# GpSimd's weight subtractions one per block of products, and zero matmuls in TensorE's idle time of the search

## The chip, the cores and the metric

The kernel runs on one core of a Trainium2 chip. The metric is the device time of one execution in microseconds (us); less is better. Engines are named as in the profile: PE is TensorE (PEld its weight loads), DVE is VectorE, ACT is ScalarE, POOL is GpSimd, SP is SyncE, which issues most of the DMAs.

## What is computed

A gated linear attention over 32 heads feeds a mixture of experts, in which tokens are assigned to experts greedily over all pairs (the reference, cut):

```python
batch, n_heads, seq, head_dim = (4, 8, 768, 48)      # 3072 tokens of 384 features
for t in range(S):
    state = alpha[:, :, t, :, None] * state + einsum('bhd,bhe->bhde', k[:, :, t], v[:, :, t])
    y[:, :, t] = einsum('bhd,bhde->bhe', q[:, :, t], state)
...
N, D, E, F = (3072, 384, 8, 1024)
logits = x @ w_gate
order = argsort(-logits.flatten())                   # best (token, expert) pairs first
for idx in order:
    tok, e = idx // E, idx % E
    if assigned[tok] >= 0 or counts[e] >= N // E:    # at most 384 tokens for each expert
        continue
    assigned[tok] = e; counts[e] += 1
for e in range(E):
    h = maximum(x[mask_e] @ w1[e], 0)                # w1[e] is 384x1024
    out[mask_e] = h @ w2[e]                          # w2[e] is 1024x384
```

## The kernel before

The program is recorded first and ordered afterwards. Each operation is handed to a `Plan` (`pl.add(engine, cost, fn, r=..., w=...)`) with an assumed cost, what it reads and what it writes. `Plan.order` lays all operations out in a simulated time by these costs, by priorities (`pl.base`: an earlier expert and an earlier block rank higher) and by buffers that come free; `Plan.issue` emits them in that order. On the chip each engine runs its own instructions strictly in the order emitted and waits on semaphores for the others. So a changed cost or a new dependency moves instructions on all engines.

The run has three stages.

1. Attention: 24 steps of four chunks of 128 tokens. The last products of a step on PE are those of the function `intra`. Behind the last step stand on PE only transposes, logits (L452, L460) and the counts of `choice` (L520).
2. Search and assignment. The greedy order is replaced by eight rounds. A round finds the next expert that becomes full, and its threshold, digit by digit. In one step of a round DVE compares the tokens' digits with all possible values (`cmp`, L638), PE counts with 24 small matmuls (L668), DVE makes `g` (L671), PE broadcasts it by one matmul (L675), DVE takes `k` (L677) and the next digit `nd` (L680). `update` (L730 to L760) then moves the tokens of the full expert to their next choice. `extract` makes the row numbers of the round's tokens (`hot` L804, PE's pick L810, `idx` L813), and POOL gathers the rows with three indirect DMAs (`xr`, L818).
3. The experts. For each of the eight experts the 1024 hidden features are done in eight blocks of 128. `prep` transposes the gathered rows on PE (L887) and splits them into a rounded part `xh` (ACT, L889) and a rest `xl` (DVE, L891). A block (`ffn1`) takes three products of three matmuls each into a PSUM tile `s` (L905; there are two of them): `w1h` with `xh`, `w1h` with `xl`, `w1l` with `xh`. ACT takes the relu (`hh`, L909), DVE its rest (`hl`, L910). `ffn2` (L927) multiplies by `w2` two blocks later, into the tiles `y`, `lg` and `xt`. The result is copied by ACT (`yo`) and scattered to the output by POOL (L937).

From the second round on, rounds and experts overlap: while the blocks of one expert run, the round of the next is searched, and on PE the counts stand between the products.

`split` prepares the weights, half an expert (four blocks) at a time. ACT rounds `w1r` to `w1h` (L861). POOL takes the rest, `w1l = w1r - w1h` (L866), in one subtraction of 128x384 elements per block, 64 in all. The rest of `w2` is made by ACT (L870) and an accumulating DMA that POOL issues (`w2l`, L874). POOL's queue thus holds the subtractions, the gathers `xr`, the `w2l` DMAs and the scatters, in one order. A subtraction may run as soon as its weights are loaded and rounded and one of three half-expert buffers of `w1l` is free. The `Plan` knows the operations marked `port=True` (the subtractions, `cmp`, `hot`): in its simulated time these never overlap.

Of the kernel before, what the change touches and what calls it, by code (L numbers as in the profile page):

```python
# [35 lines left out]
class Plan:  # L36


    def __init__(self):
        self.ops, self.writer, self.readers, self.base, self.free = [], {}, {}, 0.0, {}  # L40

# [97 lines left out]
    def issue(self):  # L139
        self.prev = {}  # L140
        for i in self.order():
            self.ops[i][2]()
            self.prev[self.ops[i][0]] = i


HOP = {"PE": 0.3, "DVE": 0.15, "ACT": 0.2, "POOL": 0.2, "SP": 2.2}
OVER, SELF = {"DVE": 0.09}, {"DVE": 0.035}
# [4 lines left out]
def gla_moe_kernel(ctx, tc, q, k, v, alpha, w_gate, w1, w2, out):  # L152
    nc = tc.nc
# [178 lines left out]
    def step(s):  # L332
# [103 lines left out]
        for a in range(2):  # L436
            def intra(a=a):
                for u in (2 * a, 2 * a + 1):
                    for h in range(2):
                        nc.tensor.matmul(yb.t[64 * h:64 * h + D, u], rv.t[:, u, h], sm.t[:, h, u],  # L440
                                         start=False, stop=(u == 3), skip_group_check=True)
            add(P_, 0.44, intra, r=[sm, rv], w=[yb], mode=48)
        add(A_, 0.6, lambda: nc.scalar.activation(yt.t, yb.t, AF.Copy), r=[yb], w=[yt])
# [181 lines left out]
    scattered, stores = [], set()  # L625
    gap = rw.tile([128, 1], F32, name="gap")

    def v_(cost, fn, r=(), w=(), port=False):
# [224 lines left out]
    def split(i, hf, raw):  # L853
# [4 lines left out]
        for a in range(2):  # L858
# [4 lines left out]
            for b in range(2):  # L863
                c2 = slice(a * w_ + b * 128, a * w_ + b * 128 + 128)
                pl.base = at(i, 4 * hf + 2 * a + b)
                add(G_, 1.08, lambda c2=c2: nc.gpsimd.tensor_sub(l1.t[:, :, c2], r1.t[:, :, c2], h1.t[:, :, c2]),  # L866
                    r=[r1, (h1, a)], w=[(l1, 2 * a + b)], port=True)
            q2 = slice(2 * a, 2 * a + 2)
# [9 lines left out]
    def prep(i, xr):  # L878
        xh, xl = pl.buf(XH), pl.buf(XL)
        pl.base = at(i) + 20.0  # L880
        for b in range(NB):
# [3 lines left out]
            def turn_rows(b=b, x=x):  # L885
                for d in range(DB):
                    nc.tensor.transpose(x.t[:, d], xr.t[:, b, d * 128:(d + 1) * 128], ident)  # L887
            add(P_, 0.33, turn_rows, r=[(xr, b)], w=[x], mode=128)
            add(A_, 0.49, lambda x=x, bs=bs: nc.scalar.activation(xh.t[:, :, bs], x.t[:, :DB], AF.Copy),  # L889
# [5 lines left out]
    def ffn1(i, q, w, xh, xl):  # L895
# [12 lines left out]
        src = lambda: o.t.rearrange("p a b -> p (a b)")[:, :CAP]  # L908
        add(A_, 0.49, lambda: nc.scalar.activation(hh.t, src(), AF.Relu), r=[o], w=[hh])  # L909
        v_(0.553, lambda: nc.vector.scalar_tensor_tensor(hl.t, src(), 0.0, hh.t, op0=OP.max, op1=OP.subtract),  # L910
# [107 lines left out]
```

## Time and profile before

| what | value |
|---|---|
| three runs | 511.98, 511.89, 509.33 us; median 511.89 |
| profiled execution, its own time | 509.61 us |
| its span, first to last instruction | 507.9 us |
| mean granted PE clock | 0.901 |
| PE / PEld / DVE busy | 412.1 / 366.4 / 301.6 us |
| ACT / POOL busy | 194.4 / 229.4 us |
| first product of an expert | 177.16 us |

Busy time is the sum of the intervals in which an engine's instructions ran; an instruction that is held up while it runs counts with its whole length. The granted clock (PEclk) is the share of full speed at which PE was allowed to run. A row of the timeline gives the start in us, the duration in us, the engine, the source line, the operation, output<-input, the shapes and how many of them stand in a row; in brackets follow the idle time of the engine before it and what ended that. A row of a group ends with the busy time in us and the mean of one in ns, and behind the bar the idle time before. A row of a table of windows gives the window, its length, the busy time and number of instructions of each engine, the granted clock, the DMAs' share and their GB/s.

### The profile page before, as it was taken

What the parts mean: (1) busy time and instruction counts of PE and PEld (TensorE: products, weight loads), DVE (VectorE), ACT (ScalarE), POOL (GpSimd) and SP (SyncE); (2) the same over time, 40 slices, a digit from 0 to 9 for tenths busy, and PEclk for the clock granted to TensorE, in tenths of its full rate; (3) what the DMA queues carried; (4) which work ended last, traced back from release to release, by engine and by line L of the source; (5) the groups of instructions that cost most, each with busy time, mean ns of one, the idle gap of its engine ahead of it and who ended that gap; (6) DMA issues with size and microseconds to landing.
All of it is one profiled execution on the core that took longest, in us unless ns stands there. A gap on an engine that the chain in (4) does not pass through costs nothing.

```text
span 507.9 us, 10573 instructions
## 1 busy us (share of the span) xinstructions
PE 412.1 (81%) x4134; PEld 366.4 (72%) x4134; DVE 301.6 (59%) x823; ACT 194.4 (38%) x351; POOL 229.4 (45%) x257
## 2 busy tenths in 40 slices
PE   4899999999832486995978868897869959889792
PEld 2778887788722375984977767796759949889691
DVE  6978878877468649558569568447666612021110
ACT  1456554555300431720631622533432434633211
POOL 5777776677100521580622920850470653630202
PEclk8799999999965559996999989899889989989997
DMA  8859977621010755943814914833841992433101
GB/s 301 307 190 310 305 233 218 174 94 64 3 63 0 203 157 124 286 109 107 255 31 122 300 22 89 317 62 63 298 107 22 318 361 63 108 63 62 48 0 46
DMA packets 37681, 76.28 MB, mean 150 GB/s; under 512 B 3584, under 2 KB 17920, under 8 KB 37632
## 3 DMA queue, kind: packets, MB, share of 16 engines
q1 hardware_dynamic: 32256, 53.60, 31.3%
q0 software_dynamic: 5376, 22.02, 18.1%
q8 instruction: 32, 0.52, 0.4%
q14 instruction: 17, 0.14, 0.1%
HBM read 53.59 MB, written 9.44 MB: 124 GB/s over the span
## 4 chain that ended last, share of the span: by engine, by line
PE 48%; DVE 23%; issue 15%; DMA 5%; POOL 5%; ACT 2%; SPq 0%; POOLq 0%; DVEq 0%; ACTq 0%
PE s L905 12%; DVE cmp L638 5%; PE s L389 4%; PE y L927 4%; PE y L440 4%; PE st L668 4%; PE y L433 3%; PE xt L377 3%; PE xt L927 3%; PE lg L927 3%; DMA xr<-x_dram,idx 3%; DMA w2r<-in_moe_w_dram 3%; PE lg L452 2%; POOL out_dram L937 2%; DVE te L349 2%
## 5 line engine op out<-in xcount | busy, mean ns | idle before, releaser
L910 DVE SCALAR_TENSOR_TENSOR hl<-s,hh 128x384 fp32r<-128x384 f32 x64 | 35.3, 554 | 93.7 <-ACT hh L909 61.4
L866 POOL TENSOR_TENSOR w1l<-w1r,w1h 128x384 fp32r<-128x384 f32 x64 | 68.1, 1242 | 37.8 <-ACT w1h L861 37.7
L909 ACT ACTIVATE hh<-s 128x384 fp32r<-128x384 f32 x64 | 31.4, 491 | 120.1 <-PE s L905 113.3
L937 POOL DMA_INDIRECT out_dram<-yo,idx x24 | 29.4, 1225 | 69.3 <-ACT yo L932 65.8
L905 PE MATMUL s<-xh,w1h 128*128 128x384 f32 x192 | 48.7, 365 | 8.3 <-DVE hl L910 5.4
L668 PEld LDWEIGHTS <-cmp 128*128 128x128 bf16 x816 | 30.5, 118 | 32.8 <-DVE cmp L638 27.0
L668 PE MATMUL st<-o,cmp 128*128 128x8 bf16 x816 | 33.1, 175 | 25.1 <-DVE cmp L638 18.2
L905 PE MATMUL s<-xh,w1l 128*128 128x384 f32 x192 | 48.8, 365 | 5.4 <-DVE hl L910 3.2
L905 PE MATMUL s<-xl,w1h 128*128 128x384 f32 x192 | 49.2, 367 | 4.7 <-ACT hh L909 2.6
L638 DVE TENSOR_TENSOR cmp<-nd,iota 128x1536 bf16<-128x1536 bf16 (+4 forms) x32 | 51.5, 1619 | 0.8
L818 POOL DMA_INDIRECT xr<-x_dram,idx x24 | 26.1, 1089 | 49.9 <-DVE idx L813 44.5
L874 POOL DMA_DIRECT2D w2l<-w2r x16 | 15.3, 956 | 73.5 <-ACT w2l L870 71.7
L905 PEld LDWEIGHTS s<-xh,w1h 128*128 128x128 f32 x192 | 36.3, 204 | 9.7 <-DVE hl L910 5.6
L905 PEld LDWEIGHTS s<-xh,w1l 128*128 128x128 f32 x192 | 36.1, 203 | 7.6 <-issue 6.5
L905 PEld LDWEIGHTS s<-xl,w1h 128*128 128x128 f32 x192 | 36.1, 204 | 7.0 <-ACT hh L909 3.9
L861 ACT ACTIVATE w1h<-w1r 128x768 fp32r<-128x768 f32 x32 | 26.0, 838 | 32.7 <-DMA w1r<-in_moe_w_dram 32.6
L359 POOL TENSOR_TENSOR kh<-rk,te 128x512 f32<-128x512 f32 (+1 forms) x24 | 29.4, 1229 | 18.0 <-DVE te L349 7.3
L389 PE MATMUL s<-qh,kh 64*128 64x128 f32 x384 | 31.0, 298 | 7.0 <-DVE qh L359 6.0
L392 POOL TENSOR_SCALAR_AFFINE_SELECT sm<-sm 128x1024 f32<-128x1024 f32 x24 | 26.8, 1116 | 17.9 <-ACT sm L391 16.3
L389 PEld LDWEIGHTS s<-qh,kh 64*128 64x128 f32 x384 | 25.0, 195 | 11.8 <-DVE qh L359 6.5
L359 POOL TENSOR_TENSOR qh<-rq,tp 128x512 f32<-128x512 f32 (+1 forms) x24 | 29.5, 1229 | 5.2 <-DVE tp L355 4.1
L349 DVE TENSOR_TENSOR_SCAN te<-al,z 128x511 f32<-128x511 f32 (+2 forms) x26 | 30.9, 1189 | 0.9
(190 smaller groups left out, 957.9 us busy)
## 6 DMA issues: line engine op xcount, KB each, us to landing
w1r<-in_moe_w_dram SPq DMA_DIRECT2D x16, 768.0 KB, 7.3
w2r<-in_moe_w_dram SPq DMA_DIRECT2D x16, 768.0 KB, 8.4
w2l<-w2r POOLq DMA_DIRECT2D x16, 768.0 KB, 6.1
al<-in_alpha_dram SPq DMA_DIRECT2D x24, 260.0 KB, 4.4
rk<-in_k_dram SPq DMA_DIRECT2D x24, 256.0 KB, 4.4
rq<-in_q_dram SPq DMA_DIRECT2D x24, 256.0 KB, 4.2
rv<-in_v_dram SPq DMA_DIRECT2D x24, 192.0 KB, 3.6
x_dram<-xg SPq DMA_DIRECT2D x6, 768.0 KB, 4.4
```

What stands on the lines that cost most here:

```text
L349: nc.vector.tensor_tensor_scan(te.t[:, lo:top][:, ::-1], al.t[:, lo + 1:top + 1][:, ::-1], zb[:, lo + 1:top + 1][:, ::-1], al.t[:, 4 * C + ...
L359: eng.tensor_tensor(out_.t[:, us].rearrange("p u c -> p (u c)"), x.t[:, lo:hi], f.t[:, lo:hi], op=OP.mult)
L389: nc.tensor.matmul(sc.t[:, h, u], kh.t[hs, u], qh.t[hs, u], start=True, stop=True)
L392: add(G_, 1.15, lambda: nc.gpsimd.affine_select(sm.t, sm.t, pattern=[[0, 8], [1, C]], compare_op=OP.is_ge, fill=0.0, base=0, channel_multi ...
L638: v_(0.12 + 0.00054 * nt * (js.stop - js.start), lambda js=js: nc.vector.tensor_tensor(words(dst, nt, js), keyed(d, nt, js), each(iotas[t] ...
L668: nc.tensor.matmul(rt[:, 32:40], dst[:, j // U, :, j % U], o[:, j], start=(j == 0), stop=(j == NU - 1))
L866: add(G_, 1.08, lambda c2=c2: nc.gpsimd.tensor_sub(l1.t[:, :, c2], r1.t[:, :, c2], h1.t[:, :, c2]), r=[r1, (h1, a)], w=[(l1, 2 * a + b)], ...
L905: nc.tensor.matmul(o.t.rearrange("p a b -> p (a b)")[:, :CAP], a.t[:, d, cs_], x.t[:, d], start=(n == 0 and d == 0), stop=(n == 2 and d == ...
L909: add(A_, 0.49, lambda: nc.scalar.activation(hh.t, src(), AF.Relu), r=[o], w=[hh])
L910: v_(0.553, lambda: nc.vector.scalar_tensor_tensor(hl.t, src(), 0.0, hh.t, op0=OP.max, op1=OP.subtract), r=[o, hh], w=[hl])
L927: nc.tensor.matmul(flat(y.t)[:, :Dm], a.t[:, bs], x.t[:, j], start=(q == 0 and n == 0), stop=(q == FB - 1 and n == 2))
L937: x = nc.gpsimd.indirect_dma_start(out=out, out_offset=bass.IndirectOffsetOnAxis(ap=idxs[i % 4][:, b:b + 1], axis=0), in_=yo.t, in_offset= ...
```

## The change

Two things are done.

First, the subtraction of block n (n counts all 64 blocks) waits for the relu of block n-6 (`GATE = 6`), by a token ("pace", n) in the Plan and by a semaphore in the program (`add_manual_dep`). The first six have no such wait. The assumed cost of a subtraction goes from 1.08 to 1.2.

Second, `Plan.issue` fills PE's planned idle time between the last `intra` and the last transpose of the first expert's rows. Ahead of each PE operation there it puts as many zero matmuls (bf16, a zero 128x128 weight and 256 zero columns, into the second tile `s`, which nothing else uses at that time) as fit into the Plan's idle time ahead of it, less 0.25, at 0.11 each. Nothing reads their result.

```diff
@@ class Plan
 
     def issue(self):
-        self.prev = {}
-        for i in self.order():
-            self.ops[i][2]()
+        self.prev, end, on = {}, 0.0, False
+        self.order()
+        for t, i in sorted(self.times):
+            eng, cost, fn = self.ops[i][:3]
+            if self.spin and eng == "PE":
+                first, last, one, each, spare = self.spin
+                on = (on or i == first) and i != last
+                if on:
+                    for _ in range(int((t - end - spare) / each)):
+                        one()
+                end = t + cost
+            fn()
             self.prev[self.ops[i][0]] = i
 
+GATE = 6
...
-            add(P_, 0.44, intra, r=[sm, rv], w=[yb], mode=48)
+            grp["intra"] = add(P_, 0.44, intra, r=[sm, rv], w=[yb], mode=48)
...
+    paced = {}
...
                 pl.base = at(i, 4 * hf + 2 * a + b)
-                add(G_, 1.08, lambda c2=c2: nc.gpsimd.tensor_sub(l1.t[:, :, c2], r1.t[:, :, c2], h1.t[:, :, c2]),
-                    r=[r1, (h1, a)], w=[(l1, 2 * a + b)], port=True)
+                n = FB * i + 4 * hf + 2 * a + b - GATE
+
+                def sub(c2=c2, n=n):
+                    x = nc.gpsimd.tensor_sub(l1.t[:, :, c2], r1.t[:, :, c2], h1.t[:, :, c2])
+                    if n >= 0:
+                        tc.add_manual_dep(x.ins, paced[n].ins.name,
+                                          mybir.DependencyInfo(mybir.DependencyClass.Sync, mybir.DependencyReason.DATA),
+                                          reason="one subtraction for each block of products")
+                add(G_, 1.2, sub, r=[r1, (h1, a)] + ([("pace", n)] if n >= 0 else []), w=[(l1, 2 * a + b)], port=True)
...
-            add(P_, 0.33, turn_rows, r=[(xr, b)], w=[x], mode=128)
+            turned = add(P_, 0.33, turn_rows, r=[(xr, b)], w=[x], mode=128)
+            if i == 0:
+                pl.spin = (grp["intra"], turned, lambda: nc.tensor.matmul(
+                    flat(HB.tiles[1])[:, :256], warm[:, :128], warm[:, :256], start=True, stop=True), 0.11, 0.25)
...
-        add(A_, 0.49, lambda: nc.scalar.activation(hh.t, src(), AF.Relu), r=[o], w=[hh])
+        def relu():
+            paced[FB * i + q] = nc.scalar.activation(hh.t, src(), AF.Relu)
+        add(A_, 0.49, relu, r=[o], w=[hh, ("pace", FB * i + q)])
```

188 zero matmuls come of it, each with its weight load, in 22 groups of 1 to 31. The largest groups stand ahead of the last counts of `choice` (21), of the matmul that ends the first round (22), and of the first counts of the second round (31); most steps of the first round have 3 ahead of the broadcast and 10 or 11 ahead of the counts. 13 stand between the second step of the second round and the first transpose of the gathered rows, and 3 more behind that.

PE, where attention ends (`yt` is an output tile of attention, `lt` the logits, `lg` their PSUM tile; L-numbers of the changed kernel are its own). Before:

```order
L440 MATMUL y<-sm_152,rv_136 48x128 x8
L377 MATMUL xt<-ident,yt_161 128x128 x4
L377 MATMUL xt<-ident,yt_162 128x128 x4
L452 MATMUL lg<-yt_162,wg 64x128 x4
L460 MATMUL xt<-ident,lt_176 128x128 x2
```

And in the changed kernel, up to the first of the zero matmuls:

```order
L450 MATMUL y<-sm_152,rv_136 48x128 x8
L387 MATMUL xt<-ident,yt_161 128x128 x4
L908 LDWEIGHTS warm
L908 MATMUL s<-warm 128x256
L387 MATMUL xt<-ident,yt_162 128x128 x4
L462 MATMUL lg<-yt_162,wg 64x128 x4
```

A weight load and a zero matmul, three times (the pair is shown once), now stand between the two transposes; seven more stand ahead of the transpose of the logits. The real instructions keep their order on PE until the first expert's products.

DVE, where the first expert's rows arrive during the second round (`xl` is the rest of the rows, one row per 128 tokens; `nd`, `cmp`, `g`, `k` are the round's). Before:

```order
L680 SCALAR_TENSOR_TENSOR nd_271<-nd_270,k_245,z 128x24
L891 TENSOR_TENSOR xl_2112<-xt,xh_2110 128x3x128
L638 TENSOR_TENSOR cmp_97<-nd_271,iota_80 128x6x256
L891 TENSOR_TENSOR xl_2112<-y,xh_2110 128x3x128
L671 TENSOR_TENSOR g_244<-st,rem 64x8
```

And in the changed kernel:

```order
L691 SCALAR_TENSOR_TENSOR nd_271<-nd_270,k_245,z 128x24
L912 TENSOR_TENSOR xl_2232<-xt,xh_2230 128x3x128
L912 TENSOR_TENSOR xl_2232<-y,xh_2230 128x3x128
L649 TENSOR_TENSOR cmp_97<-nd_271,iota_80 128x6x256
L933 SCALAR_TENSOR_TENSOR hl_2238<-s,hh_2234 128x384
```

The last `xl` (from the tile `y`) has moved ahead of the comparison, and a rest `hl` of the first block now stands between the comparison and `g`.

POOL, around the fourth expert's weights (`w1l0` and `w1l1` are its two halves, `w1l2` the first half of the fifth; `xr0` with `idx0` is the gather for the fifth expert). Before:

```order
L874 DMA w2l0_2105<-w2r2_2094 128x1536
L866 TENSOR_TENSOR w1l0_2099<-w1r2_2090,w1h0_2096 128x3x128 x3
L866 TENSOR_TENSOR w1l1_2100<-w1r3_2091,w1h1_2097 128x3x128 x4
L874 DMA w2l1_2106<-w2r3_2095 128x1536
L937 DMA out_0_dram<-yo1_2123,idx2_275 3072x384
L936 MEMSET gap_278 128x1
L937 DMA out_0_dram<-yo2_2124,idx2_275 3072x384
L866 TENSOR_TENSOR w1l2_2101<-w1r0_2088,w1h2_2098 128x3x128
L818 DMA xr0_2108<-x_dram_62,idx0_273 128x384 x3
```

In the changed kernel, first the subtractions:

```order
L892 DMA w2l0_2225<-w2r2_2214 128x1536
L880 TENSOR_TENSOR w1l0_2219<-w1r2_2210,w1h0_2216 128x3x128 x3
L880 TENSOR_TENSOR w1l1_2220<-w1r3_2211,w1h1_2217 128x3x128
L892 DMA w2l1_2226<-w2r3_2215 128x1536
L880 TENSOR_TENSOR w1l1_2220<-w1r3_2211,w1h1_2217 128x3x128 x2
L960 DMA out_0_dram<-yo1_2243,idx2_275 3072x384
```

and two scatters later the gather:

```order
L959 MEMSET gap_278 128x1
L960 DMA out_0_dram<-yo3_2245,idx2_275 3072x384
L880 TENSOR_TENSOR w1l1_2220<-w1r3_2211,w1h1_2217 128x3x128
L829 DMA xr0_2228<-x_dram_62,idx0_273 128x384 x3
L880 TENSOR_TENSOR w1l2_2221<-w1r0_2208,w1h2_2218 128x3x128
```

The run of seven subtractions is broken up by the `w2l` DMA and the three scatters, and each of them now waits for its own relu; the gather for the fifth expert stands behind the fourth expert's last subtraction, which waits for the relu of that expert's second block, where before it stood behind the fifth expert's first.

More of the change, by code (lines that the diff above doesn't have):

```diff
@@ L39, in __init__ @@
     def __init__(self):
-        self.ops, self.writer, self.readers, self.base, self.free = [], {}, {}, 0.0, {}
+        self.ops, self.writer, self.readers, self.base, self.spin = [], {}, {}, 0.0, None
     def buf(self, kind):
```

## The prediction

> **What bounds the kernel now.** I read the granted clock by slices first, then a table of windows from the end of attention on, then what PE waited for while experts and rounds overlap, and last the timeline at the longest of these waits.
>
> ```profile
> PEclk8799999999965559996999989899889989989997
> ```
>
> The clock is near full except in one long valley (slices of 12.7 us; the valley begins at about 140 us) and some short ones.
>
> ```profile
> core 0: us, PE busy (x) PEld busy (x) DVE busy (x) ACT busy (x) POOL busy (x), PEclk, DMA share, GB/s
> 139.40:144.20 4.80, 1.23 (x15) 0.52 (x9) 2.55 (x16) 0.66 (x2) 0.00 (x0) 1.00 0.45 164
> 144.20:157.60 13.40, 4.87 (x100) 4.23 (x101) 9.31 (x34) 0.00 (x0) 0.00 (x0) 0.50 0.00 1
> 157.60:173.10 15.50, 4.00 (x78) 3.45 (x77) 12.12 (x41) 3.73 (x5) 2.92 (x3) 0.50 0.39 118
> 177.10:192.00 14.90, 13.32 (x81) 11.11 (x82) 7.46 (x13) 5.50 (x10) 5.52 (x7) 0.50 0.61 160
> 192.00:202.20 10.20, 5.80 (x51) 5.04 (x50) 9.72 (x43) 0.86 (x2) 0.69 (x1) 1.00 0.46 98
> 272.00:278.00 6.00, 4.00 (x42) 3.52 (x41) 5.78 (x21) 1.97 (x4) 1.79 (x1) 1.00 0.34 101
> ```
>
> The clock falls at 144.2 us after PE was busy 1.23 of 4.80 us, stays at half through the first rounds (busy 4.87 of 13.40 and 4.00 of 15.50), and still for the first 14.9 us of the experts, where PE is nearly always busy (13.32). Busy shares of 57% and 67% (the last two rows) kept full clock. So the first experts' products run at half speed because the rounds ahead of them left PE idle.
>
> ```profile
> PE st L668 <- DVE cmp L638: 11.4, 4, 4.5
> PE y L927 <- DVE hl L910: 6.5, 3, 2.5
> PE s L905 <- DVE hl L910: 4.8, 2, 4.1
> PE xt L887 <- DMA xr<-x_dram,idx: 0.9, 1, 0.9
> ```
>
> From 206 to 398 us (rows: us in total, times, longest) PE waits most for comparisons, then for `hl`, which stands behind them on DVE, and hardly for gathered rows. What makes a comparison late:
>
> ```profile
> 249.63 7.21 POOL L866 TENSOR_TENSOR w1l<-w1r,w1h 128x384 fp32r<-128x384 f32 x7
> 252.87 4.79 DVE L638 TENSOR_TENSOR cmp<-nd,iota 128x1536 bf16<-128x1536 bf16 x1
> 288.57 7.17 POOL L866 TENSOR_TENSOR w1l<-w1r,w1h 128x384 fp32r<-128x384 f32 x7
> 290.32 6.23 DVE L638 TENSOR_TENSOR cmp<-nd,iota 128x1536 bf16<-128x1536 bf16 x1
> 296.61 0.96 PE L668 MATMUL st<-o,cmp 128*128 128x8 bf16 x24 [3.99 <-DVE cmp L638]
> 190.24 2.50 DVE L688 TENSOR_SCALAR ab<-nd,k 128x24 f32<-128x24 bf16 x1
> 190.42 2.27 POOL L866 TENSOR_TENSOR w1l<-w1r,w1h 128x384 fp32r<-128x384 f32 x2
> ```
>
> Twice a comparison begins inside a run of seven subtractions on POOL and ends 0.8 us after that run. A comparison of this shape that meets none takes under 1 us, as the groups by shape (from 140 us on) tell:
>
> ```profile
> L638 DVE TENSOR_TENSOR cmp<-nd,iota 128x1536 bf16<-128x1536 bf16 x14 | 31.2, 2233 | 0.3
> L638 DVE TENSOR_TENSOR cmp<-nd,iota 128x1560 bf16<-128x1560 bf16 x6 | 5.8, 969 | 0.2
> L638 DVE TENSOR_TENSOR cmp<-nd,iota 128x3072 bf16<-128x3072 bf16 x6 | 11.4, 1898 | 0.2
> L638 DVE TENSOR_TENSOR cmp<-d,iota 128x3072 bf16<-128x3072 bf16 x6 | 10.5, 1748 | 0.0
> L688 DVE TENSOR_SCALAR ab<-nd,k 128x24 f32<-128x24 bf16 x7 | 3.9, 552 | 0.0
> ```
>
> The 14 comparisons of the first row cost 31.2 us where the second row's price makes 14 x 0.97 = 13.6: 17.6 us lost. The third against the fourth loses 6 x 0.15 = 0.9 us, and the `ab` at 190.24 some 2.2 us. Together 20.7 us in which DVE stood locked behind POOL.
>
> **The change part by part.** The sum goes against the profiled execution's 509.6 us (span 507.9, 1.7 us around it), which lies 2.3 us under the median of 511.9.
>
> *Zero matmuls in the rounds.* They have to hold the clock, and they stand in front of real work.
>
> ```profile
> 150.60 1.03 PE L668 MATMUL st<-o,cmp 128*128 128x8 bf16 x24 [1.13 <-DVE cmp L638]
> 210.55 0.80 PE st L668 x24
> 1.40 3.74 PE y L308 x10
> 140.22 0.44 PE L460 MATMUL xt<-ident,lt 128*128 128x128 f32 x2 [0.48 <-ACT lt L461]
> 168.59 0.96 PE L668 MATMUL st<-o,cmp 128*128 128x8 bf16 x24 [1.58 <-DVE cmp L638]
> 173.13 0.87 PE L887 MATMUL xt<-ident,xr 128*128 128x128 f32 x3 [3.16 <-DMA xr<-x_dram,idx]
> ```
>
> 24 counts take 1.03 us at half clock and 0.80 at full (chain of waits). In four steps of the first round only the half behind the second comparison is exposed (4 x 0.12), in two of the second all of it (2 x 0.23): -0.9 us. A zero matmul with 256 columns is bounded above by half a 512-column warm-up matmul at low clock, 374/2 = 187 ns, below by a full-clock share of it, about 100 ns; at full clock I take 0.11. Then 7 of them (0.8 us) fill a gap of 0.48 us ahead of L460, and 14 (1.5) one of 1.58 ahead of a count: +0.3 us. Were the clock low all the same, the 188 would take 35 us in gaps made for 21, and some 6 us of that would show. Together -1 us (bounds -2 to +6).
>
> *Start of the experts.* If the clock is full at 177 us, the 13.32 us of PE in the window to 192 become 6.7.
>
> ```profile
> 187.45 1.33 PE L905 MATMUL s<-xh,w1h 128*128 128x384 f32 x3 [0.84 <-DVE hl L910]
> 192.98 0.68 PE L905 MATMUL s<-xh,w1h 128*128 128x384 f32 x3
> 176.54 2.78 DVE L638 TENSOR_TENSOR cmp<-nd,iota 128x1536 bf16<-128x1536 bf16 x1
> 179.25 0.55 DVE L891 TENSOR_TENSOR xl<-y,xh 128x384 fp32r<-128x384 f32 x1
> ```
>
> Three matmuls took 1.33 us there and 0.68 once the clock was back. Most of it is on the path, since the broadcasts of the second round stand in PE's queue behind these products. The last `xl`, which ended late at 179.8 behind a comparison of 2.78 us, now goes ahead of it. DVE's 7.46 us and the waits for `hl` become the next limit, so I take -5 us (bounds 0 and -6.7).
>
> *Subtractions spread out.* POOL's work stays 64 subtractions. Before 400 us about 52 of them, at 1.0 us unhindered, still cover about a fifth of the 224 us, so of some 38 operations of DVE that can be locked (comparisons, `hot`, `ab`) I expect 8 to 10 to meet one or two subtractions, 0.7 us each: 7 us in place of 20.7. Of the 14 us less, the share on the path is read from the waits: 11.4 us of PE's waiting for 20.7 lost, 0.55, so -8 us. Two of the long waits also cost the clock:
>
> ```profile
> 296.00:302.00 6.00, 5.39 (x42) 4.94 (x43) 3.58 (x8) 0.49 (x1) 0.00 (x0) 0.72 0.00 0
> 380.00:386.00 6.00, 6.00 (x34) 5.35 (x33) 2.65 (x6) 1.47 (x3) 0.00 (x0) 0.74 0.01 3
> ```
>
> 0.28 x 5.39 + 0.26 x 6.00 = 3.1 us, of which I take -2. Bounds of this part: 0 (as many collisions as before) to -17 (none, all on the path).
>
> The Trainium skill, SBUF — State Buffer, section "Who interferes with whom", says that DVE with two SBUF inputs and a reading GpSimd instruction exclude each other, and that whoever starts first holds the port for its whole instruction. By that rule a comparison would wait for one subtraction, 1 us, however many stand in a row, and this part would be worth nothing. The trace differs: 6.23 us behind a run of seven.
>
> *The new waits on POOL.* Behind a subtraction that waits for its relu stand the gathers, the `w2l` DMAs and the scatters. No product waits for a paced subtraction: its third product comes six blocks later, over 18 us. The gathers can lose.
>
> ```profile
> 323.13 1.01 POOL L818 DMA_INDIRECT xr<-x_dram,idx  x1 [0.17 <-issue]
> 329.64 0.49 ACT L909 ACTIVATE hh<-s 128x384 fp32r<-128x384 f32 x1 [4.04 <-PE s L905]
> 283.27 0.47 ACT L909 ACTIVATE hh<-s 128x384 fp32r<-128x384 f32 x1
> 284.07 4.17 DMA xr<-x_dram,idx
> ```
>
> The relu that the fifth expert's gather will wait for came at 329.64, that gather at 323.13. But the pick of its rows also moves behind that block on PE. For the fourth expert the relu (283.27) and the gather (landing on the chain from 284.07) fall together. Each of seven gathers can lose up to a subtraction, 1.0 to 1.4 us; I take +2 us (bounds 0 and +10). `w2l` and scatters had waited 70 us in all and cover theirs.
>
> *Sum:* -1 -5 -8 -2 +2 = -14: 495.6 for the profiled execution, 498 from the median. I say 497.
>
> **The rivals.**
> - *The clock is lost at the gather.* The last big group of zero matmuls (13, 1.4 us) ends about 1.7 us ahead of the rows' landing, and only transposes follow. If that lets the clock fall, the first 3 us or more run at half speed, and the 5 us shrink to 1: 501. The share of busy time (over 50%) speaks against it. The Trainium skill, TensorE: Matmul & The Clock Gate, Part 4, says that transposes do not count as busy; the trace before cannot tell.
> - *The spreading pays nothing.* If subtractions in ones and twos meet as many operations as the runs did, the 10 us go: 507. For it: they now lie in every stretch. Against: a run of seven holds DVE once for over 5 us.
> - *All of it is on the path*, and no gather is late: 489.
> - *POOL's queue becomes the bound, slower.* If the paced subtractions ahead of the gathers of experts four to eight put each off by the 6.5 us between 323.13 and 329.64, and 1.5 of them are hidden (an estimate), five times 5 us stand against the sum's 16 without the +2: +9, or 519. It decides where rows land over 3 us, on average, after PE has come to their transposes. For it: each such gather now stands behind a wait. Against: PE waited for rows 0.9 us in all from 206 to 398 us, so gathers have had slack.
> - *Nothing moves:* the new order gives back elsewhere what it takes, 510.
>
> **How the numbers follow.** Forecast 497 (from 490 to 503): 0.47; clock lost, 501: 0.15; all on the path, 489: 0.08; spreading pays nothing, 507: 0.10; nothing moves, 510: 0.09; POOL the bound, 519: 0.11. A change under 0.5% (2.6 us) can hardly be told from none here. Faster: 0.47 + 0.15 + 0.08 + 0.07 of the 507 case = 0.77; same: 0.12; slower: 0.11. The range leaves out most of the slow case and the lowest end: 487 to 511.
>
> **What would show it.** Right: full clock from 144 to 190 us and products of 0.5 us per three from the start; no comparison over 2.5 us; PE's wait for comparisons under 5 us; the first product of an expert 1 to 2 us earlier. Wrong: half clock in the first experts, counts that wait for zero matmuls, gathers that start behind a waiting subtraction while PE waits for `xr`, or comparisons of 2 to 3 us in greater number.

## The result and the profile after

The changed kernel takes 492.27 us in the median of three runs (489.76 to 495.42) against 511.89: a ratio of 0.9636 with a 95% interval of [0.9536, 0.9737]. In six further runs (`after_again`, below) it is 0.9643 [0.9585, 0.9701]. An execution more than 1.5% above the fastest of its kernel counts as slow: ratios with an interval leave such executions out, medians and ratios without an interval take them all, and the profiled executions of `spread_only`, `cost_only`, `gate4` and `gate12` were slow in this sense. The profiled execution took 492.27 us, with a span of 490.6 and a mean granted clock of 0.947, against 509.61, 507.9 and 0.901 before: 17.3 us less. Line numbers are ten to twenty-odd higher than before: `cmp` is L649, the counts L679, the subtractions L880, the zero matmuls L908, `xl` L912, the products L926, the relu L931, `hl` L933, the second products L950.

The granted clock by slices and a table of windows (columns as before):

```profile
PEclk8799999999999979899799899899989979999996
```
```profile
core 0: us, PE busy (x) PEld busy (x) DVE busy (x) ACT busy (x) POOL busy (x), PEclk, DMA share, GB/s
144.20:157.60 13.40, 13.30 (x180) 10.64 (x179) 9.04 (x33) 0.00 (x0) 0.00 (x0) 1.00 0.00 1
157.60:172.49 14.89, 12.03 (x154) 9.58 (x151) 12.96 (x44) 2.13 (x3) 1.68 (x2) 1.00 0.34 109
172.49:175.90 3.41, 1.80 (x32) 1.73 (x33) 0.62 (x2) 2.98 (x5) 3.09 (x4) 1.00 0.55 154
175.90:182.80 6.90, 6.27 (x23) 5.33 (x20) 3.07 (x5) 0.98 (x2) 3.55 (x4) 0.51 0.88 175
182.80:192.00 9.20, 7.49 (x78) 6.33 (x77) 3.66 (x12) 5.87 (x9) 2.39 (x3) 1.00 0.58 178
```

The long valley is gone: the clock stays full through the rounds. It is lost at the gather all the same, right behind the 3.41 us in which PE was busy 1.80, and comes back at 182.8 us, not at 192.0. But the rounds did not become faster, and the first product stands at 178.09 us (177.16 before). The counts of the rounds take as long at full clock as at half. The first row is the group of them in the kernel before (144.2 to 173.1 us, clock 0.50), the second in the changed kernel (144.2 to 172.4 us, clock 1.00); then follow a group of zero matmuls and the first products:

```profile
L668 PE MATMUL st<-o,cmp 128*128 128x8 bf16 x144 | 6.1, 175 | 10.7 <-DVE cmp L638 6.8 <-DVE o L760 3.9
L679 PE MATMUL st<-o,cmp 128*128 128x8 bf16 x144 | 6.1, 175 | 0.9 <-DVE o L771 0.7
```
```profile
150.31 1.27 PE L908 MATMUL s<-warm 128*128 128x256 bf16 x10
178.09 2.29 PE L926 MATMUL s<-xh,w1h 128*128 128x384 f32 x6 [0.58 <-ACT xh L910]
```

What PE waited for from 206 to 400 us (us in total, times, longest): no comparison is left among the first rows, where 11.4 us stood.

```profile
PE s L926 <- DVE hl L933: 6.2, 4, 4.1
PE s L926 <- ACT hh L931: 5.7, 6, 1.4
PE xt L905 <- DMA xr<-x_dram,idx: 4.7, 2, 4.3
PE y L950 <- DVE hl L933: 2.9, 2, 1.5
```

The groups by shape (140 us on) and a stretch of the timeline in which subtractions come singly; the second starts 0.15 us behind the end of the relu that lets it go (relu at 260.52 for 0.49, subtraction at 261.16):

```profile
L649 DVE TENSOR_TENSOR cmp<-nd,iota 128x1536 bf16<-128x1536 bf16 x14 | 15.2, 1094 | 0.4
L880 POOL TENSOR_TENSOR w1l<-w1r,w1h 128x384 fp32r<-128x384 f32 x64 | 68.2, 1120 | 112.1 <-ACT hh L931 76.3 <-ACT w1h L872 31.6 <-issue 4.0
```
```profile
256.56 1.02 POOL L880 TENSOR_TENSOR w1l<-w1r,w1h 128x384 fp32r<-128x384 f32 x1 [2.73 <-issue]
258.69 0.97 DVE L649 TENSOR_TENSOR cmp<-nd,iota 128x1560 bf16<-128x1560 bf16 x1
260.52 0.49 ACT L931 ACTIVATE hh<-s 128x384 fp32r<-128x384 f32 x1 [2.24 <-PE s L926]
261.16 1.00 POOL L880 TENSOR_TENSOR w1l<-w1r,w1h 128x384 fp32r<-128x384 f32 x1 [2.75 <-ACT hh L931]
```

Not all are single: three runs of three (at 176, 216 and 250 us) and one of four (at 190 us) are left. The 14 comparisons cost 15.2 us in place of 31.2. Counted over every operation of DVE after 176 us (its time less the shortest of the same line, operation, tiles and shape, where that is over 0.25 us), DVE was lengthened by 6.4 us; by this count it was 21.8 before. I call this "lengthened" below.

Where the time came from is read off the starts of the relus. Expert 0, block 7: 218.88 before, 214.88 after (-4.0). Block 7 of experts 1, 2, 4 and 7: -6.4, -11.1, -18.1, -16.8. So some 4 us come in the first expert and some 14 from then to the fifth, of which about 1 is lost again by the eighth.

### The profile page after: what moved, and what is told of

Read it like the earlier page. It is cut to its first block, busy times and chain, and to the rows that moved or that the text cites. A ratio compares the mean times of both kernels' runs of the same rounds, so it can differ in the third digit from the quotient of the medians.

```text
span 490.6 us, 10942 instructions
## 1 busy us (share of the span) xinstructions
PE 428.2 (87%) x4322; PEld 379.3 (77%) x4322; DVE 287.5 (59%) x823; ACT 194.3 (40%) x351; POOL 226.6 (46%) x256
## 4 chain that ended last, share of the span: by engine, by line
PE 51%; DVE 17%; issue 11%; DMA 11%; POOL 5%; ACT 2%; SPq 1%; POOLq 0%; DVEq 0%; ACTq 0%
PE s L926 13%; DMA w2r<-in_moe_w_dram 5%; PE s L399 4%; PE st L679 4%; PE y L950 4%; PE lg L950 4%; PE y L450 4%; PE xt L950 4%; PE y L443 4%; PE xt L387 3%; DMA xr<-x_dram,idx 3%; DVE cmp L649 2%; DMA rq<-in_q_dram 2%; PE lg L462 2%; POOL w1l L880 2%
## 5 line engine op out<-in xcount | busy, mean ns | idle before, releaser
L880 POOL TENSOR_TENSOR w1l<-w1r,w1h 128x384 fp32r<-128x384 f32 x64 | 68.2, 1120 | 112.1 <-ACT hh L931 76.3
L933 DVE SCALAR_TENSOR_TENSOR hl<-s,hh 128x384 fp32r<-128x384 f32 x64 | 35.5, 555 | 95.4 <-ACT hh L931 61.5
L931 ACT ACTIVATE hh<-s 128x384 fp32r<-128x384 f32 x64 | 31.4, 491 | 126.9 <-PE s L926 117.6
L926 PE MATMUL s<-xh,w1h 128*128 128x384 f32 x192 | 47.7, 360 | 12.2 <-DVE hl L933 7.5
L926 PE MATMUL s<-xh,w1l 128*128 128x384 f32 x192 | 48.1, 360 | 6.8 <-DVE hl L933 3.2
L926 PE MATMUL s<-xl,w1h 128*128 128x384 f32 x192 | 48.7, 364 | 4.3 <-ACT hh L931 2.9
L926 PEld LDWEIGHTS s<-xh,w1h 128*128 128x128 f32 x192 | 35.3, 198 | 14.4 <-DVE hl L933 8.4
L960 POOL DMA_INDIRECT out_dram<-yo,idx x24 | 25.5, 1065 | 42.3 <-ACT yo L955 39.4
L926 PEld LDWEIGHTS s<-xh,w1l 128*128 128x128 f32 x192 | 35.7, 200 | 8.9 <-issue 5.0
L926 PEld LDWEIGHTS s<-xl,w1h 128*128 128x128 f32 x192 | 35.6, 201 | 6.8 <-ACT hh L931 3.9
L369 POOL TENSOR_TENSOR kh<-rk,te 128x512 f32<-128x512 f32 (+1 forms) x24 | 29.4, 1227 | 18.1 <-DVE te L359 12.7
L679 PEld LDWEIGHTS <-cmp 128*128 128x128 bf16 x816 | 30.4, 118 | 6.9 <-issue 4.7
L649 DVE TENSOR_TENSOR cmp<-nd,iota 128x1536 bf16<-128x1536 bf16 (+4 forms) x32 | 34.9, 1101 | 0.8
L402 POOL TENSOR_SCALAR_AFFINE_SELECT sm<-sm 128x1024 f32<-128x1024 f32 x24 | 26.7, 1114 | 18.1 <-ACT sm L401 16.6
L399 PEld LDWEIGHTS s<-qh,kh 64*128 64x128 f32 x384 | 24.9, 194 | 11.7 <-DVE qh L369 6.7
L679 PE MATMUL st<-o,cmp 128*128 128x8 bf16 x816 | 33.1, 175 | 0.9 <-DVE o L771 0.7
L365 DVE TENSOR_TENSOR_SCAN tp<-al,z 128x512 f32<-128x512 f32 (+1 forms) x26 | 29.6, 1137 | 0.2
## 6 DMA issues: line engine op xcount, KB each, us to landing
rv<-in_v_dram SPq DMA_DIRECT2D x24, 192.0 KB, 3.8
```

Source lines behind the costliest of these rows:

```text
L365: nc.vector.tensor_tensor_scan(tp.t[:, lo:hi], al.t[:, lo:hi], zb[:, lo:hi], 1.0, op0=OP.mult, op1=OP.add)
L369: eng.tensor_tensor(out_.t[:, us].rearrange("p u c -> p (u c)"), x.t[:, lo:hi], f.t[:, lo:hi], op=OP.mult)
L399: nc.tensor.matmul(sc.t[:, h, u], kh.t[hs, u], qh.t[hs, u], start=True, stop=True)
L402: add(G_, 1.15, lambda: nc.gpsimd.affine_select(sm.t, sm.t, pattern=[[0, 8], [1, C]], compare_op=OP.is_ge, fill=0.0, base=0, channel_multi ...
L649: v_(0.12 + 0.00054 * nt * (js.stop - js.start), lambda js=js: nc.vector.tensor_tensor(words(dst, nt, js), keyed(d, nt, js), each(iotas[t] ...
L679: nc.tensor.matmul(rt[:, 32:40], dst[:, j // U, :, j % U], o[:, j], start=(j == 0), stop=(j == NU - 1))
```

## The experiments

The table gives each run's profiled execution in three numbers (granted clock in the rounds at 145 to 172 us; the time from the first gather's start to the relu of expert 0, block 5; the lengthened time of DVE) and its times. The ratio is to the kernel before in the same call; on the chip of the four runs marked * that took 527.88 us in the median, so they are compared by ratio alone. Where runs lay too far apart for an interval the ratio is that of the medians.

| kernel | clock | gather to relu 0.5 | lengthened | median us | ratio |
|---|---|---|---|---|---|
| before | half | 40.5 | 21.8 | 511.89 | 1 |
| changed | full | 36.0 | 6.4 | 492.27 | 0.9636 [0.9536, 0.9737] |
| after_again | full | 35.0 | 8.1 | 494.84 | 0.9643 [0.9585, 0.9701] |
| spread_only | half | 35.4 | 10.5 | 496.38 | 0.966 |
| spin_only | full | 40.1 | 19.6 | 514.73 | 1.0051 [1.0008, 1.0095] |
| order_no_wait | full | 36.1 | 14.1 | 496.06 | 0.9714 [0.9658, 0.9769] |
| hold_clock | full | 36.3 | 6.3 | 491.75 | 0.9602 [0.9550, 0.9654] |
| cost_only * | half | 35.4 | 26.0 | 519.83 | 0.985 |
| pause_before * | half | 40.9 | 29.7 | 534.71 | 1.0215 [1.0132, 1.0298] |
| gate4 * | full | 35.0 | 10.6 | 498.97 | 0.947 [0.9306, 0.9635] |
| gate12 * | full | 35.8 | 24.9 | 516.22 | 0.978 |
| w1l_by_dma | full | 44.7 | 0 | 498.96 | 0.9689 [0.9631, 0.9747] |
| spin_all | full | 34.8 | 6.9 | 492.08 | 0.9577 [0.9516, 0.9638] |
| first_on_pool | full | 34.9 | 2.6 | 496.99 | 0.9716 [0.9656, 0.9776] |

**Each part alone.** `spread_only` leaves `pl.spin` unset. `spin_only` is this:

```diff
-GATE = 6
+GATE = 1000
-                add(G_, 1.2, sub, ...
+                add(G_, 1.08, sub, ...
```

> Leaves out the zero matmuls, keeps the paced subtractions and their order. Theory (the spreading brings most of the gain, because DVE is no longer locked behind runs of subtractions, and the zero matmuls bring only the earlier return of the clock at the first expert): half clock again from about 144 to 190 us, the first relus 3 to 4 us later than in the changed kernel, comparisons as short as there; 496 us (494 to 499), ratio to before 0.97. Rival (the clock carries the gain): 505 us or more.

> Only the zero matmuls on the kernel before; subtractions in runs as before. Theory: full clock to about 176 us, but the first gather no earlier than before; the first expert's first eight relus 2 to 4 us earlier, after which the runs of subtractions lock DVE as before (lengthened operations near 20 us): 508 us (506 to 510), ratio 0.993. Rival (the clock carries the gain): 498 us or less.

```profile
144.20:157.60 13.40, 13.31 (x178) 10.54 (x177) 9.21 (x34) 0.00 (x0) 0.00 (x0) 1.00 0.01 1
177.10:192.00 14.90, 11.78 (x85) 10.31 (x85) 8.80 (x16) 6.43 (x10) 5.82 (x7) 0.73 0.62 162
```
```profile
177.24 2.50 DVE L649 TENSOR_TENSOR cmp<-nd,iota 128x1536 bf16<-128x1536 bf16 x1
179.65 0.54 DVE L912 TENSOR_TENSOR xl<-y,xh 128x384 fp32r<-128x384 f32 x1
196.16 0.49 ACT L931 ACTIVATE hh<-s 128x384 fp32r<-128x384 f32 x1 [4.72 <-PE s L926]
206.03 0.49 ACT L931 ACTIVATE hh<-s 128x384 fp32r<-128x384 f32 x1 [0.20 <-ACT w2h L890]
```

These rows are of `spin_only`; the next is of `spread_only`:

```profile
177.10:192.00 14.90, 13.18 (x95) 11.43 (x95) 6.62 (x16) 6.48 (x11) 5.13 (x6) 0.78 0.78 191
```

In `spin_only` the clock is full through the rounds, and the fourth and fifth relu come at 196.16 and 206.03 as before the change (196.28 and 206.02): the zero matmuls alone gain nothing and cost up to 1%. My theory, which gave them 2 to 4 us in the first expert, is wrong there. In `spread_only` the rounds run at half clock, and the same two relus come at 192.75 and 198.53, about as early as in the changed kernel (192.92 and 198.25). So the first expert's gain does not come from the clock in the rounds. It does not come from the clock behind them either. That was higher in all three than before the change: from 177.1 to 192 us it was 0.50 before, 0.81 in the changed kernel, 0.78 in `spread_only` and 0.73 in `spin_only`. But the last two hardly differ in it and lie 4.7 us apart in the first expert (35.4 and 40.1 us).

The 496.38 us of `spread_only` lie 4.6 us over `hold_clock` in the same call. But its profile has a comparison held for 4.55 us too, by a run of three at 251.62, two of whose gates had opened 9.1 and 3.4 us before, and one of its six runs took 486.99 us, less than any of `hold_clock` (487.58 to 492.88). So what the zero matmuls bring beside the spreading is not settled: between nothing and some 5 us.

**The order.** `cost_only` is the kernel before with 1.08 made 1.2, nothing else.

> The kernel before with one number changed: the planner's price of a subtraction 1.2 in place of 1.08; no pacing, no zero matmuls. On DVE its order is that of the changed kernel up to the third expert (the last xl of the first expert ahead of the comparison too), on POOL it still has runs of three to four. Theory (the first expert's gain comes from that order, not from the clock; the gain after it comes from shorter runs): clock low from 144 to about 190 us as before, yet the relu of expert 0, block 7 at 214.5 to 216 us (before 218.9); lengthened DVE operations 12 to 18 us in all, 503 us (498 to 507). Rival (the gain of the first expert needs the clock): that relu at 218 us or later, 508 us.

The first expert's gain is there, with half clock in the rounds and with POOL in runs (35.4 us from gather to relu 0.5). Here too the clock came back early (0.89 from 177.1 to 192 us), but in `spin_only` 0.73 brought only 0.4 us. What makes the gain is the order that the Plan drew up, on two engines; how much each of the two brings was not separated. On DVE the last `xl` goes ahead of the comparison. On PE, before the change, the counts stood ahead of block 4's products and waited 2.92 us for the round's `o`, and the products then took their turn (timeline of the kernel before). In the changed kernel that block's products stand ahead of them and are done in time for a relu at 198.25 (second fence):

```profile
201.49 0.94 PE L668 MATMUL st<-o,cmp 128*128 128x8 bf16 x24 [2.92 <-DVE o L760]
202.83 1.33 PE L905 MATMUL s<-xh,w1h 128*128 128x384 f32 x3 [0.40 <-DVE hl L910]
206.02 0.49 ACT L909 ACTIVATE hh<-s 128x384 fp32r<-128x384 f32 x1 [0.57 <-ACT w2h L872]
```
```profile
197.45 0.70 PE L926 MATMUL s<-xh,w1l 128*128 128x384 f32 x3
198.25 0.49 ACT L931 ACTIVATE hh<-s 128x384 fp32r<-128x384 f32 x1 [4.84 <-PE s L926]
203.31 0.99 PE L679 MATMUL st<-o,cmp 128*128 128x8 bf16 x24
```

After that `cost_only` loses again: POOL still has runs of seven, and PE waits 21.4 us for comparisons from 206 to 400 us. The longest hold in its timeline:

```profile
299.18 7.11 POOL L866 TENSOR_TENSOR w1l<-w1r,w1h 128x384 fp32r<-128x384 f32 x7
299.84 7.27 DVE L638 TENSOR_TENSOR cmp<-nd,iota 128x1536 bf16<-128x1536 bf16 x1
307.16 0.96 PE L668 MATMUL st<-o,cmp 128*128 128x8 bf16 x24 [6.73 <-DVE cmp L638]
```

The comparison came 0.66 us into the run and ended 0.82 us after it; in the kernel before another came later into its run and was held 6.23 us. Its six runs went from 494.65 to 530.97 us. That fits a cost which hangs on the moment of arrival, but only one of these runs has a profile.

**The order without the wait.**

```diff
-                    if n >= 0:
+                    if False:
                         tc.add_manual_dep(x.ins, paced[n].ins.name, ...
```

> The changed kernel's order on every engine, instruction for instruction, without the subtractions' wait for a relu (no product needs it). Theory (the wait is what spreads them; without it POOL takes them as soon as their weights are there, up to the next instruction in its queue that waits for something else): subtractions again in runs of three and more, lengthened DVE operations 12 to 20 us, 503 us (499 to 508). Rival (the order alone does it, since gathers and w2l DMAs stand between them): 492 us, like the changed kernel, with lengthened operations near 6 us.

The order on every engine is that of the changed kernel, and 18.7 us of medians separate it from `spin_only`, which has zero matmuls as well. So most of the gain is the Plan's new order. With it PE waits hardly any longer for comparisons from 206 to 400 us, where 11.4 us stood before and 7.5 in `spin_only`:

```profile
PE st L679 <- DVE cmp L649: 2.0, 3, 1.0
```

That is 9.4 us less than before; with the 2.8 us that the first expert gains here (relu 0.7 at 216.06 in place of 218.88), it makes about the 12.0 us between the profiled executions (509.61 and 497.66). In the new order `w2l` DMAs and gathers stand between the subtractions. That this is what shortens the waits is argued; no run tests it apart from the rest of the order. It does not spread them fully. The timeline still has runs of four, and a comparison that comes late into one:

```profile
286.65 4.35 POOL L880 TENSOR_TENSOR w1l<-w1r,w1h 128x384 fp32r<-128x384 f32 x4
289.63 2.20 DVE L649 TENSOR_TENSOR cmp<-nd,iota 128x1536 bf16<-128x1536 bf16 x1
```

Lengthened time is 14.1 us in place of 6.4. The wait itself is worth about 4 us: `hold_clock`, which has it, took 491.75 in the same call, and the two intervals (0.9658 to 0.9769, 0.9550 to 0.9654) just do not meet. The two kernels differ by 14 zero matmuls too, and the interval of the changed kernel itself, from another call (0.9585 to 0.9701), does overlap that of `order_no_wait`. So the 4 us are an estimate.

**The distance.** `gate4` and `gate12` set `GATE` to 4 and 12.

> The changed kernel with the gate four blocks back in place of six. Subtractions come two blocks earlier to their products' deadline wait: they would start 8 to 9 us later than in the changed kernel, still more than 5 us ahead of their products. Theory (only that they come singly counts): 492 us (490 to 495), lengthened DVE operations 5 to 8 us. Rival (the distance matters, since later subtractions push the gathers, w2l DMAs and scatters behind them): 496 us or more.

> The changed kernel with the gate twelve blocks back: a subtraction may come six blocks earlier. Theory (only that they come singly counts, but with twelve blocks the weights' arrival and free buffers, not the relu, release many, so that runs come back in part): lengthened DVE operations 8 to 14 us, 495 us (492 to 499). Rival (the order alone carries the gain): 492 us, as with six.

With twelve blocks POOL has runs of seven again, the same lengths of runs as in `cost_only`; DVE is lengthened by 24.9 us, PE waits 21.7 us for comparisons from 206 to 400 us, and 0.978 is left, more than I expected to lose. With four, 48 of the 64 subtractions stand alone (43 with six), and DVE is lengthened by 10.6 us, more than the 5 to 8 expected. I expected 492 us and got 499 on a chip where everything was slower; by the ratio the interval overlaps that of six. Whether four beats six stays open, since the two were not run on the same chip.

**Does a pause let DVE in?**

```diff
                 def sub(c2=c2):
                     nc.gpsimd.tensor_sub(l1.t[:, :, c2], r1.t[:, :, c2], h1.t[:, :, c2])
+                    nc.gpsimd.memset(gap, 0.0)
```

> The kernel before with a tiny memset of one column on POOL behind every subtraction, in the same order. Tells whether POOL's hold on DVE passes from one subtraction straight to the next, or is given up for whatever DVE has waiting as soon as POOL does something else in between. Theory (POOL holds DVE through a whole run because its next subtraction asks before the first ends): with an operation in between that does not need it, DVE gets in after one subtraction; lengthened operations fall from 21.8 us to under 8, 500 us (496 to 504). Rival (DVE is locked by the sheer share of POOL's time, or the memset holds it as well): 20 us or more lengthened as before, and 512 to 518 us, since the memsets lengthen POOL's queue.

```profile
215.68 0.95 POOL L818 DMA_INDIRECT xr<-x_dram,idx  x1 [0.30 <-issue]
216.39 8.99 DVE L638 TENSOR_TENSOR cmp<-nd,iota 128x1536 bf16<-128x1536 bf16 x1
216.64 1.01 POOL L867 TENSOR_TENSOR w1l<-w1r,w1h 128x384 fp32r<-128x384 f32 x1
217.58 0.12 POOL L868 MEMSET gap<- 128x1 f32 x1
217.63 1.00 POOL L867 TENSOR_TENSOR w1l<-w1r,w1h 128x384 fp32r<-128x384 f32 x1
...
223.18 1.37 POOL L867 TENSOR_TENSOR w1l<-w1r,w1h 128x384 fp32r<-128x384 f32 x1
```

The gain did not come. Seven subtractions with a memset behind each, and a `w2l` DMA issued among them, held one comparison for 8.99 us, and DVE was lengthened by 29.7 us. But the memset makes no pause: the second subtraction starts at 217.63, 0.02 us before the first one ends (216.64 for 1.01). So the theory's reason, that the next subtraction asks before the first ends, is not refuted. Whether a real pause lets DVE in, this run does not say, except that the 0.62 us which the DMA puts between the fourth and the fifth subtraction did not.

The comparison had even begun 0.25 us ahead of the first subtraction. The Trainium skill, SBUF — State Buffer, section "Who interferes with whom", says that whoever issues first has the shared pair for its whole instruction and the other blocks; by that rule this comparison should have gone through. But POOL was still issuing a gather at that moment (first row). Later in the same run a comparison began 0.23 us ahead of a subtraction while POOL stood at a wait:

```profile
361.56 0.95 DVE L638 TENSOR_TENSOR cmp<-nd,iota 128x1536 bf16<-128x1536 bf16 x1
361.79 1.59 POOL L867 TENSOR_TENSOR w1l<-w1r,w1h 128x384 fp32r<-128x384 f32 x1 [1.96 <-ACT w1h L861]
```

There the comparison took its 0.95 us, and the subtraction, 1.0 us by itself, took 1.59. In the fourteen profiles together, eight comparisons began less than 0.8 us ahead of a subtraction with no instruction of POOL under way, and none was lengthened. Fifteen began so while POOL issued a gather, a scatter or a `w2l` DMA; eleven of them were lengthened, and why the other four were not stays open. So the "first" of the rule holds here where POOL had stood still. Its "whole instruction" is too short: a run of subtractions keeps DVE out until its end.

In the changed kernel only 8 of the 27 comparisons after 176 us meet a subtraction at all, and two of these, both inside a run of three, are lengthened (by 0.8 and 1.2 us). In the eight cases POOL had stood still for 1.3 us or more when the comparison began; how short a standstill is enough was not tried.

**No subtraction on POOL at all.** In `w1l_by_dma` ACT writes minus the rounded part, and a DMA adds the weights:

```diff
-            for b in range(2):
-                ... tensor_sub(l1, r1, h1) on POOL
+            add(A_, 0.84, lambda c=c: nc.scalar.activation(l1.t[:, :, c], r1.t[:, :, c], AF.Copy, scale=-1.0), ...
+        add(G_, 1.0, lambda: nc.gpsimd.dma_start(l1.t.bitcast(F32), r1.t, accum_op=OP.add, ...
```

> The changed kernel with no subtraction on POOL at all: ACT writes the negative of the rounded part (32 more activations of 0.84 us), and one accumulating DMA for each half of an expert's weights adds the weights to it, as is done for w2l. Theory (the lock by POOL's subtractions is what costs): lengthened DVE operations fall from 6.4 to under 2 us, and the time by another 2 to 4 us to 488 or 490, unless ACT's 27 us more make relus late. Rival (the subtractions cost through POOL's queue or port in other ways, and with them gone the gathers, scatters and w2l DMAs come earlier too): 485 us or less. Other way: ACT becomes the limit, 497 us or more.

Not one operation of DVE is lengthened any more, which shows the subtractions as the cause of that (POOL still issues its gathers, scatters and DMAs); yet it is slower than the changed kernel by 4 us of medians. In the first expert the first relu comes 7 us later than in the changed kernel, and ACT's timeline tells why:

```profile
178.31 0.49 ACT L902 ACTIVATE xh<-y 128x384 fp32r<-128x384 f32 x1 [0.41 <-PE y L897]
189.27 0.84 ACT L878 ACTIVATE w2l<-w2r 128x768 fp32r<-128x768 f32 x1 [10.46 <-DMA w2r<-in_moe_w_dram]
190.75 0.47 ACT L923 ACTIVATE hh<-s 128x384 fp32r<-128x384 f32 x1
```

The new plan put a `w2l` copy, whose weights were still under way, ahead of the first relu in ACT's queue. `first_on_pool` (subtractions on POOL for expert 0 alone) was still built on another reading, that products waited for the accumulating DMA:

> The changed kernel with the subtractions of the first expert on POOL as there, and those of the other seven done by ACT and accumulating DMAs (as in the run before for all eight). Theory (that run lost 12 us in the first expert, whose third products waited for accumulating DMAs, and gained later because nothing locks DVE): relu of expert 0, block 7 at 214 to 216 us as in the changed kernel, lengthened DVE operations 2 to 5 us, all in the first expert, time 487 us (484 to 491), under the changed kernel. Rival (ACT's extra work and the DMAs make up for the lock gone): 492 to 496 us.

Its first expert is back (34.9 us), 2.6 us are lengthened, and it still takes 497 us. From 216 to 315 us PE waits there for `hl` and for a round's `o`:

```profile
PE s L933 <- DVE hl L940: 5.1, 3, 4.1
PE y L957 <- DVE hl L940: 3.6, 1, 3.6
PE st L679 <- DVE o L771: 3.5, 1, 3.5
```

The last two rows have no counterpart in the changed kernel, where `y` waited at most 1.5 us for `hl` and no wait for `o` is listed. That DVE's new order puts other work ahead of them, and that these waits use up what the missing lock gains, is argued and not tested. What is shown is that neither of the two kernels turned the last 6 us of collisions into time.

**More clock.** `hold_clock` puts 14 zero matmuls ahead of the first transposes. `spin_all` does this too, and fills PE's planned idle time up to the end with 126 more of 128 columns.

> The changed kernel with 14 more zero matmuls (1.6 us at full clock) ahead of the first transposes, where PE waits 1.6 us for the first gather. Theory (the clock falls at 175.9 us because PE is idle at the gather and only transposes follow): full clock through 175.9 to 182.8 us, first expert's relus 2 to 3 us earlier, 489.5 us (488 to 491). Rival (the transposes lose the clock all the same, or DVE's hl is the limit there): half clock again from about 176 to 183 us, and 492 us.

> The changed kernel with 14 more zero matmuls ahead of the first transposes and 126 of 128 columns in PE's planned idle time after them, up to the end. Theory (the clock is no limit where DVE's chain or a gather is waited for): the granted clock rises from 0.947 to about 0.97, the time falls by at most 2 us, 490 us. Rival (half clock in the seven stretches after 175 us, 34 us in all, costs half of it): 480 us or less. Other way: the zero matmuls stand ahead of real work and cost 2 us or more.

```profile
176.00:178.00 2.00, 0.07 (x1) 0.00 (x0) 0.87 (x3) 0.25 (x1) 2.00 (x4) 1.00 0.75 143
178.00:180.00 2.00, 1.41 (x6) 1.18 (x7) 0.89 (x2) 0.49 (x1) 1.07 (x2) 0.68 1.16 197
```

In `hold_clock` (windows above) the clock fell 3 us later, at 178.7 us: the third part of the gather came 1.4 us later than in the changed kernel, and PE stood still from 176 to 178 us. Its time is that of the changed kernel within the intervals. In `spin_all` the clock stayed full until 187.6 us, and the first six products (L939 there) took 1.34 us in place of 2.29:

```profile
177.10:183.00 5.90, 4.83 (x54) 4.51 (x55) 3.65 (x7) 1.02 (x3) 3.07 (x4) 1.00 0.92 166
```
```profile
178.85 1.34 PE L939 MATMUL s<-xh,w1h 128*128 128x384 f32 x6
```

Yet its time from gather to relu 0.5 is 34.8 us, against 35.0 in `after_again` in the same call, whose clock was half from 177.2 to 184.0 us. The mean clock rose from 0.947 to 0.975, and the time is again the same: 492.08 against 494.84, with intervals that overlap, and profiled executions of 490.53 and 490.19.

> The changed kernel itself, beside the next two and in more runs: 492 us where the kernel before takes 512, ratio 0.95 to 0.97. If what a run of subtractions costs hangs on the moment at which a comparison comes to it, the kernel before varies from chip to chip and run to run by more than the changed one does.

The kernel before varied in that call from 507.33 to 517.22 us, the changed one from 490.19 to 500.12: no steadier. That part of the expectation is not borne out.

## Why the prediction was right, and where its steps were not

The forecast of 497 (487 to 511) against a measured 492.27 holds, and so does its direction. Term by term, against the profiled executions (-14 predicted, -17.3 measured):

- *Zero matmuls in the rounds, -1:* alone they cost 0.1 to 1%, some 0.4 to 5 us (`spin_only`), within the bounds of -2 to +6. The price was right: ten took 1.27 us, and less the 0.27 us of a single one that is 0.11 for each of the other nine. The gain was not. The step that failed is "24 counts take 1.03 us at half clock and 0.80 at full": 1.03 is a row of the timeline, and 0.80 a piece of the chain of waits, which leaves out what overlaps the piece ahead of it. In the timeline 24 counts whose comparisons are both ready take 0.96 us at half clock (168.59 us, before) and 0.96 at full (256.20 us, after), so there was nothing to gain.
- *Start of the experts, -5:* 4.5 us were gained there (40.5 to 36.0 us from gather to relu 0.5), by another cause; that the size came out is luck. The step that failed is that a full clock at 177 us makes 6.7 us of PE's 13.32, and that most of this is on the path. The condition did not hold, since the clock was half from 175.9 to 182.8 us. Where it did hold, in `spin_all`, it was worth 0.2 us (34.8 against 35.0). The new order with a clock of 0.78 gave 35.4 us, the old order with 0.73 gave 40.1. I named the moved `xl` and gave it nothing of its own; the products that moved ahead of the waiting counts I overlooked.
- *Subtractions spread out, -8 and -2:* some 13 us came. The lengthened time went to 6.4 us as predicted (7). Mis-sized was the share on the path: 15.4 us fewer gave 13, so about 0.8 and not 0.55. PE's own waiting for comparisons, from which I took it, leaves out the waits for `hl` that a late comparison causes behind it, and what the new order moved besides; these two were not told apart. Nor is lengthened time a good measure of it: in `order_no_wait` it is only 7.7 us less than before, and the profiled execution is 12.0 us shorter. And the wait, which I took for the means, carries only about 4 us: the order that the Plan made of the new token and price carries the rest. The Plan and the semaphore should have been costed apart.
- *New waits on POOL, +2:* no loss shows, though the chain of waits of the changed kernel runs through a waiting subtraction ahead of two gathers (at 315.25 and 381.49 us). PE's longest wait for gathered rows is 4.3 us, and in the kernel before one of 4.0 stood at the same expert.

Of the rivals, the lost clock came true in its mechanism, at 175.9 us, and not in its price: holding the clock longer, to 178.7 us in `hold_clock` and to 187.6 in `spin_all`, gained nothing that could be measured. The Trainium skill, TensorE: Matmul & The Clock Gate, Part 4, on which it leaned, is neither borne out nor refuted: the 3.41 us before the fall had transposes in them, but also 1.6 us without any work. Of the signs, no comparison over 2.5 us and no waiting for comparisons were right; full clock to 190 us, products of 0.5 us per three from the start, and a first product 1 to 2 us earlier were wrong.

## What to carry to other kernels

Where two engines exclude each other, look for runs: an instruction that meets a run of the other engine's waits for the whole run, and a short operation behind each instruction did not break the run, since the next one started before the last had ended, while waits in the queue did. When a change goes through a planner, run its order without its waits and its waits without its fillers before crediting any of them; here the order carried most of it. Compare two times of the same thing in one kind of view only: a piece of a chain of waits is shorter than the row of the timeline that it comes from. A higher clock is worth time only where TensorE is what is waited for: 0.028 more of granted clock bought nothing that could be measured here.

## What was not expected of the hardware

- A run of subtractions on POOL keeps a comparison on DVE out until the run ends: 8.99 us for 0.95 us of work, through seven subtractions, the memsets behind them and a DMA issue. This one had begun 0.25 us before the first subtraction, while POOL issued a gather; none of the eight that began ahead of a subtraction with POOL at a standstill was held.
- The counts, matmuls of 8 columns each with its own weight load, run no faster at full clock: 144 of them average 175 ns each and 6.1 us in all at 0.50 and at 1.00.
- The clock can be lost though PE was not idle: it fell behind 3.41 us in which PE was busy for 1.80.
